# Batch 0's output projection in blocks of 384 and 192 tokens instead of two of 288

## The chip, the core and the metric

One core of a Trainium2 chip runs the whole program. The metric is device time in microseconds of one execution. The engines named below are PE (TensorE: matrix multiplies; its weight loads have a row of their own, PEld), DVE (VectorE), ACT (ScalarE), POOL (GpSimd) and SP (SyncE, which here only issues DMAs).

## The reference: what is computed

For 8 batches of 576 tokens, 8 heads and head width 64, attention reads a memory of 32 slots; the 4608 rows that come out go through a feed-forward network without a bias:

```
a      = softmax(phi over the 32 slots)
k_m    = a^T k,  v_m = a^T v            # per batch and head: 32 x 64
attn   = softmax(q k_m^T / 8) v_m       # 576 x 64 per head, 8 heads -> rows of 512
out    = ((attn @ w1) * (attn @ w2)) @ w3 @ w_out     # 512 -> 1024 -> 1024 -> 512
```

The output is float32, 4608 x 512; the kernel writes it transposed, as `outT` of 512 x 4608.

## The kernel before, in words

**Weights.** `w3` and `w_out` are multiplied together at the start (`product`, L435), so that one matrix of 1024 x 512 is left behind the product of the two first layers. It is held as a high and a low part in reduced float32, `Wh` and `Wl`.

**A batch** has two stages. In the first (`ab_unit`, L550 to L561; tokens A, a and g of the order strings) PE makes both first layers of one block of 128 features for one half of 288 tokens with 12 matmuls, ACT copies one of them out of PSUM (`a_sb`) and DVE multiplies the other with it into the tile `g`. There are 16 such units. In the second stage PE multiplies the result by `Wh` and `Wl`. For that each piece of `g` is split: ACT rounds it to the high part `sh` (token h, `high_part`, L589) and DVE subtracts to get the low part `sl` (token l, `low_part`, L595). Four buffers each of `sh` and `sl` are used in turn.

**Batch 0's second stage** is of another form than that of batches 1 to 7, and is the place of the change. It is made of 16 calls of `plain_unit` (token Q, L631), here called Q0 to Q15. Q0 to Q7 make the first half of the tokens, Q8 to Q15 the second; in each half the even ones make output rows 0 to 255 and the odd ones rows 256 to 511. A call is 12 matmuls: two column blocks of 128, two blocks of features, and three products each (`Wh` with `sh`, `Wl` with `sh`, `Wh` with `sl`). Every matmul loads 128 x 128 weights and streams 288 tokens past them. The first half accumulates in the two pairs of PSUM banks called ab, which attention also borrows, the second half in the pairs o and x. Tokens d0 to d3 (`plain_result`, L642) copy the four results out of PSUM on ACT into a tile `c` (3 buffers) and store it with one DMA from SP (`store`, L648).

**The order** is written out by hand: the strings FIRST (batch 0), SECOND and BATCH give the order in which steps are recorded, and every engine executes its own instructions in that order. Between the calls Q of batch 0 stand the steps of batch 1's attention: turn (PE transposes, L187, L190), mem (L206, L215), block (PE transposes, L234), M0 to M3 (products of the memory with `w1` and `w2`, L328, with Mh on ACT, L339, and Ml on DVE, L344), sc0 and sc1 (scores, L254), then a softmax on DVE and ACT up to `ah` and `al` (L298, L302), which batch 1's first stage reads. Behind Q15 come M2 (L328), then batch 1's first units. The buffer of PSUM that a step gets is picked when the program is made.

**SP's queue** is one line: it issues a DMA only when the tile to be stored is ready or the buffer to be filled is free, and what is behind it waits. Around d0 to d3 it holds the stores, the load of `kv` for batch 2 (four DMAs, L134 and L140) and that of `q` (L145).

Of the kernel before, what the change touches and what calls it, by code (L numbers as in the profile page):

```python
# [8 lines left out]
F32 = mybir.dt.float32  # L9
F32R = mybir.dt.float32r  # L10
# [4 lines left out]
ALU = mybir.AluOpType  # L15
# [14 lines left out]
FIRST = """  # L30
phi A a g A C1 M1 C2 C2 a g Mh1 Ml1 C3 C4 A A a g C1 a C5 g C4 C3 A A C5 a g C2 C1 a g M2 Mh2 C3 A a C4 Ml2 C1 g A C2
a C5 C4 A a g D0 A C3 g C5 A a g q h0 l0 kv Dt0 a g E0 M3 Mh3 Ml3 D1 Et0 F0 D3 A a Dt1 g D2 E1 A A Dt2 a g Et1 F1 E2 A
a g h1 l1 A a h3 g a g Et2 h2 l2 Dt3 Q E3 Q Q Et3 top h4 l3 Q l4 Q exp norm h5 Q l5 h6 turn0 l6 turn4 turnc4 Q turnc0
mem memc Q h7 l7 d0 Q kv block F3 d1 Q F2 blockc M0 b1 a0 sc0 scc0 mx0 Mh0 sb0 ex0 Ml0 Q Q Q M1 a2 sc1 Q sm0 mu0 Mh1
scc1 q a3 b0 tr0 ah0 Q Q d2 al0 a1 d3 Ml1
"""
# [20 lines left out]
def memory_attention__then__bilinear_ffn_kernel(  # L57
# [21 lines left out]
    nc = tc.nc  # L79
    P = 128  # L80
    B, NG, _, S = qT.shape
# [8 lines left out]
    HALF = S // 2  # L90
# [22 lines left out]
    def pair_ab():  # L113
        return ps_ab.tile([P, 2, 512], F32, name="ab")
# [328 lines left out]
    OH = DO // 2  # L443
# [91 lines left out]
    big = ctx.enter_context(tc.tile_pool(name="big", bufs=1, reuse_waits="tile"))  # L535
# [44 lines left out]
    order = (1, 4, 2, 6, 5, 7, 3)  # L580
    weights = {1: (0, 0), 5: (0, 1), 2: (1, 0), 3: (1, 1), 7: (2, 0), 6: (2, 1), 4: (3, 0)}
    sources = {1: (0, 0), 2: (0, 1), 6: (1, 1), 5: (0, 0), 7: (1, 0), 3: (0, 1), 4: (1, 1)}

    plain = ((0, 0), (0, 1), (1, 0), (1, 1))

    def high_part(b, m, G):
        src = G[sources[order[m // 2]] if b else plain[m // 2]][:, m % 2 * 2 : m % 2 * 2 + 2]
        hi = big.tile([P, 2, HALF], F32R, name="sh", tag="sh", bufs=4)
        nc.scalar.copy(out=hi, in_=src)  # L589
        G["X", m] = [hi, None, src]  # L590

    def low_part(b, m, G):
        hi, _, src = G["X", m]
        lo = G["X", m][1] = big.tile([P, 2, HALF], F32R, name="sl", tag="sl", bufs=4)
        nc.vector.tensor_tensor(out=lo, in0=src, in1=hi.bitcast(F32), op=ALU.subtract)  # L595

    def out_unit(b, m, G):
# [21 lines left out]
    def plain_unit(m, G):  # L619

        block, oh = m // 2, m % 2
        n, part = block // 4, block % 4
        if part == 0:
            G["C", n, oh] = (pair_o, pair_x)[oh]() if n else pair_ab()
        hi, lo, _ = G["X", block]
        for j in range(2):
            oc = slice(oh * OH + j * P, oh * OH + (j + 1) * P)
            for k in range(2):
                f = 2 * part + k
                for t, (x, y) in enumerate(((Wh, hi), (Wl, hi), (Wh, lo))):  # L630
                    nc.tensor.matmul(  # L631
                        G["C", n, oh][:, j, :HALF],
                        lhsT=x[f // half][:, f % half, oc],
                        rhs=y[:, k],
                        start=f == 0 and t == 0,
                        stop=f == NF - 1 and t == 2,
                    )

    def plain_result(i, G):
        n, oh = i // 2, i % 2  # L640
        c = big.tile([P, 2, HALF], F32, name="c", tag="c", bufs=3)
        nc.scalar.copy(out=c, in_=G["C", n, oh][:, :, :HALF])  # L642
        store(0, n, oh, c)

    def store(b, n, oh, c):
        at = b * S + n * HALF
        dst = outT[oh * OH : (oh + 1) * OH, at : at + HALF].rearrange("(j p) s -> p j s", j=2)
        nc.sync.dma_start(out=dst, in_=c)  # L648
# [21 lines left out]
    def batches():  # L670

        nonlocal n_o
        for b in range(B):
# [11 lines left out]
            for what in tokens((FIRST, SECOND, BATCH)[min(b, 2)]):  # L685
# [5 lines left out]
                elif what == "O":  # L691
                    out_unit(b, n_o, G)
                    n_o += 1
                elif what == "Q":
                    plain_unit(n_o, G)
                    n_o += 1
                elif what in at_stage:
                    next(next(at_stage[what]))
                elif key in ("M", "Mh", "Ml"):
                    at = b if in_a else b + 1  # L700
                    if at < B:
                        steps[at][what](pair_o if in_a and b else spare_bank(b, in_a))
                elif what in LOADS:
                    load(what + ("1" if what == "phi" or in_a else "2"), b)
                elif key == "h":
                    high_part(b, int(digit), G)
                elif key == "l":
                    low_part(b, int(digit), G)
                elif key == "f":
                    first_sum(int(digit), G)  # L710
                elif key == "S":
                    sums(what, G)
                elif key == "d":
                    plain_result(int(digit), G)
                elif what in ("p1", "p4", "p5", "u2"):
                    keep(what, G)
                elif key == "C":
                    result(b, what, G)
                elif key[0] == "-" or what in steps[0]:
                    at = b if key[0] == "-" else b + 1  # L720
                    if at < B:
                        steps[at][what.lstrip("-")](spare_bank(b, in_a))
                else:
                    weights_of_out(key, int(digit))
# [51 lines left out]
```

## Time and profile before

| | us |
|---|---|
| median of 3 runs (lowest, highest) | 541.66 (541.65, 544.39) |
| the profiled execution, its own time | 544.74 |
| its span, first to last instruction | 543.0 |
| mean granted TensorE clock | 0.993 |
| PE busy | 524.4 |
| PE weight loads busy | 445.5 |
| DVE, ACT, POOL busy | 358.8, 276.9, 127.7 |

The page is one execution. Busy time of PE counts pipelined matmuls whose durations overlap: a row's mean duration (about 295 ns for 288 tokens) is longer than the distance from one to the next. The chain of waits follows the work that ended last back through whatever released it, and gives stretches with their start and length. A timeline row has the start, the duration, engine, line, operation, output and inputs, shapes, a count, and in brackets the idle time before it with what ended that. Rows of SP's queue are marked SPq; the DMA view gives the time from a DMA's issue to its landing.

### The profile page before, as it was taken

The numbers are of one execution on the slowest core, as the hardware profiler recorded it, in microseconds if no ns is written. First come the engines' busy times: TensorE is split into PE (matmuls) and PEld (weight loads), VectorE is DVE, ScalarE is ACT, GpSimd is POOL, SyncE is SP. The second block draws the span as 40 slices with busy tenths as digits, with TensorE's granted clock in tenths as the row PEclk, the third lists the DMA queues.
The fourth block names the chain that finished last, engine by engine and source line by source line (L and its number), as shares of the span: only waits on it lengthen the run. The fifth ranks groups of instructions, "written<-read, shape, count | busy, mean of one in ns | idle before, by whom it ended". The sixth has DMA issues, their size and how long they took to land.

```text
span 543.0 us, 10835 instructions
## 1 busy us (share of the span) xinstructions
PE 524.4 (97%) x4528; PEld 445.5 (82%) x4528; DVE 358.8 (66%) x588; ACT 276.9 (51%) x469; POOL 127.7 (24%) x142
## 2 busy tenths in 40 slices
PE   2998998999999999999999999999999999999997
PEld 1444457898899898989998899889997989899996
DVE  4874958863654895389555975498548853896464
ACT  5887528644655534555354544453455345553342
POOL 0005000110163702070015302350217020800180
PEclk9997999999999999999999999999999999999999
DMA  8999712704511323043305330531123310011001
GB/s 313 404 409 357 293 43 78 262 0 164 187 45 74 125 80 118 1 176 125 95 1 175 110 109 2 174 112 66 45 91 120 140 45 1 2 45 45 1 23 65
DMA packets 28303, 64.12 MB, mean 118 GB/s; under 512 B 1632, under 2 KB 9824, under 8 KB 28256
## 3 DMA queue, kind: packets, MB, share of 16 engines
q1 hardware_dynamic: 28256, 63.45, 33.4%
q8 instruction: 35, 0.57, 0.4%
q14 instruction: 12, 0.10, 0.1%
HBM read 54.00 MB, written 9.44 MB: 117 GB/s over the span
## 4 chain that ended last, share of the span: by engine, by line
PE 89%; DMA 7%; ACT 2%; DVE 1%; SPq 1%; issue 0%
PE ab L550 37%; PE x L610 13%; PE o L610 13%; PE ab L610 4%; DMA kv<-in_kv 3%; PE ab L328 3%; PE x L435 3%; PE o L328 3%; PE o L435 3%; PE ab L631 2%; PE x L206 2%; DMA raw<-in_w_out 2%; PE ab L254 2%; PE x L631 1%; PE o L631 1%; DMA raw<-in_w3T 1%
## 5 line engine op out<-in xcount | busy, mean ns | idle before, releaser
L550 PE MATMUL ab<-ah,mh 128*128 128x288 f32 x512 | 154.6, 302 | 1.8 <-DVE ml L344 1.8
L550 PE MATMUL ab<-al,mh 128*128 128x288 f32 x512 | 151.1, 295 | 0.0
L550 PE MATMUL ab<-ah,ml 128*128 128x288 f32 x512 | 151.1, 295 | 0.0
L561 DVE TENSOR_TENSOR g<-ab,a_sb 128x288 f32<-128x288 f32 x128 | 58.0, 453 | 104.8 <-ACT a_sb L559 103.8
L550 PEld LDWEIGHTS ab<-ah,mh 128*128 128x128 f32 x512 | 96.2, 188 | 18.3 <-DVE g L561 8.5
L559 ACT COPY a_sb<-ab 128x288 f32<-128x288 f32 x128 | 50.9, 398 | 109.4 <-PE ab L550 105.9
L595 DVE TENSOR_TENSOR sl<-g,sh 128x576 fp32r<-128x576 f32 x106 | 86.6, 831 | 20.1 <-ACT sh L589 19.9
L550 PEld LDWEIGHTS ab<-al,mh 128*128 128x128 f32 x512 | 96.3, 188 | 0.2 <-issue 0.2
L550 PEld LDWEIGHTS ab<-ah,ml 128*128 128x128 f32 x512 | 96.3, 188 | 0.0
L589 ACT CAST sh<-g 128x576 fp32r<-128x576 f32 x106 | 71.0, 675 | 44.4 <-PE x L610 17.9
L566 POOL TENSOR_TENSOR g<-g,g 128x288 f32<-128x288 f32 x28 | 22.2, 807 | 155.0 <-DVE g L561 154.7
L574 POOL TENSOR_TENSOR g<-g,g 128x288 f32<-128x288 f32 x28 | 28.1, 1023 | 107.0 <-ACT a_sb L559 80.5
L610 PE MATMUL o<-sh,Wh 128*128 128x288 f32 x168 | 50.6, 301 | 0.0
L610 PE MATMUL x<-sh,Wh 128*128 128x288 f32 x168 | 50.5, 300 | 0.0
L610 PE MATMUL o<-sh,Wl 128*128 128x288 f32 x168 | 49.6, 295 | 0.0
L610 PE MATMUL x<-sh,Wl 128*128 128x288 f32 x168 | 49.6, 295 | 0.0
L610 PE MATMUL x<-sl,Wh 128*128 128x288 f32 x168 | 49.6, 295 | 0.0
L610 PE MATMUL o<-sl,Wh 128*128 128x288 f32 x168 | 49.5, 295 | 0.0
L435 PE MATMUL ab<-wo,w 128*128 128x512 f32 x64 | 29.8, 621 | 10.0 <-DVE wo L424 10.0
L610 PEld LDWEIGHTS x<-sh,Wh 128*128 128x128 f32 x168 | 31.6, 188 | 7.0 <-issue 7.0
L610 PEld LDWEIGHTS o<-sh,Wh 128*128 128x128 f32 x168 | 31.6, 188 | 3.6 <-issue 3.6
L435 PEld LDWEIGHTS ab<-wo,w 128*128 128x128 f32 x64 | 12.5, 201 | 25.3 <-issue 14.3
(139 smaller groups left out, 951.8 us busy)
## 6 DMA issues: line engine op xcount, KB each, us to landing
kv<-in_kv SPq DMA_DIRECT2D x16, 1024.0 KB, 7.4
q<-in_qT SPq DMA_DIRECT2D x8, 1152.0 KB, 5.9
outT<-c SPq DMA_DIRECT2D x32, 288.0 KB, 2.3
raw<-in_w3T SPq DMA_DIRECT2D x7, 1024.0 KB, 14.8
ph<-in_phiT SPq DMA_DIRECT2D x8, 576.0 KB, 3.8
raw<-in_w SPq DMA_DIRECT2D x4, 1024.0 KB, 18.2
raw<-in_w_out SPq DMA_DIRECT2D x3, 1024.0 KB, 10.4
kv<-in_w SPq DMA_DIRECT2D x3, 1024.0 KB, 10.9
```

Source lines behind the costliest of these rows:

```text
L206: nc.tensor.matmul(ps[h * M : (h + 1) * M, t, : 2 * D], lhsT=v["a"][:, i, t, h * M : (h + 1) * M], rhs=kvt[i][:, (4 * t + h) * 2 * D : (4 ...
L328: nc.tensor.matmul(ps[g * M : (g + 1) * M, t], lhsT=vm[b % 2][d, g], rhs=w12_sb[q][d, :, g], start=True, stop=True,)
L435: nc.tensor.matmul(pw[r][i], lhsT=x[:, i * P : (i + 1) * P], rhs=wos[k // half][:, k % half], start=k == 0, stop=k == NF - 1,)
L550: nc.tensor.matmul(both[:, w, :HALF], lhsT=x[:, t, w, fc : fc + P], rhs=y[:, n, t * HALF : (t + 1) * HALF], start=i == 0, stop=i == len(to ...
L559: nc.scalar.copy(out=a_sb, in_=both[:, 0, :HALF])
L561: nc.vector.tensor_tensor(out=G[n, f // half][:, f % half], in0=both[:, 1, :HALF], in1=a_sb, op=ALU.mult)
L566: nc.gpsimd.tensor_tensor(out=low, in0=top, in1=low, op=ALU.subtract)
L574: gp(out=s2, in0=s2, in1=s3, op=ALU.subtract)
L589: nc.scalar.copy(out=hi, in_=src)
L595: nc.vector.tensor_tensor(out=lo, in0=src, in1=hi.bitcast(F32), op=ALU.subtract)
L610: nc.tensor.matmul(ps[:, j, :HALF], lhsT=x[s][:, 2 * part + k, jc], rhs=y[:, k], start=i in (1, 4, 2, 5) and part == 0 and k == 0 and t == ...
L631: nc.tensor.matmul(G["C", n, oh][:, j, :HALF], lhsT=x[f // half][:, f % half, oc], rhs=y[:, k], start=f == 0 and t == 0, stop=f == NF - 1 ...
```

## The change

Batch 0's second stage is cut after 384 tokens instead of after 288. Q0 to Q7 stream 384 tokens in each matmul, Q8 to Q15 stream 192. The number of matmuls and of weight loads stays 192.

The first stage still makes `g` in halves of 288 tokens. So each of the first four pieces of `sh` and `sl` is now put together from two sources, 288 tokens of the first half and 96 of the second, with two instructions on ACT and two on DVE instead of one each; the last four pieces hold 192 tokens and take one each. The buffers of `sh` and `sl` are 384 wide in all batches; batches 1 to 7 use 288 of each 384.

The results are copied and stored one column block of 128 rows at a time: eight copies on ACT (four of 384, four of 192) and eight DMAs (192 KB and 96 KB) instead of four copies of 576 and four DMAs of 288 KB. The three buffers of `c` remain. In FIRST the step h3 moves behind two g, since it now reads what they write.

```diff
-a g h1 l1 A a h3 g a g Et2 h2 l2 Dt3 Q E3 Q Q Et3 top h4 l3 Q l4 Q exp norm h5 Q l5 h6 turn0 l6 turn4 turnc4 Q turnc0
+a g h1 l1 A a g a g h3 Et2 h2 l2 Dt3 Q E3 Q Q Et3 top h4 l3 Q l4 Q exp norm h5 Q l5 h6 turn0 l6 turn4 turnc4 Q turnc0
...
-    plain = ((0, 0), (0, 1), (1, 0), (1, 1))
+    WIDE = 384
+
+    def plain_parts(m, G):
+
+        fh, ks = m % 4 // 2, slice(m % 2 * 2, m % 2 * 2 + 2)
+        if m < 4:
+            return [(0, G[0, fh][:, ks]), (HALF, G[1, fh][:, ks, : WIDE - HALF])]
+        return [(0, G[1, fh][:, ks, WIDE - HALF :])]
 
     def high_part(b, m, G):
...
+        if b == 0:
+            parts = plain_parts(m, G)
+            hi = big.tile([P, 2, WIDE], F32R, name="sh", tag="sh", bufs=4)
+            for at, src in parts:
+                nc.scalar.copy(out=hi[:, :, at : at + src.shape[2]], in_=src)
+            G["X", m] = [hi, None, parts]
+            return
...
     def low_part(b, m, G):
...
+            for at, x in src:
+                x_at = slice(at, at + x.shape[2])
+                nc.vector.tensor_tensor(out=lo[:, :, x_at], in0=x, in1=hi[:, :, x_at].bitcast(F32), op=ALU.subtract)
+            return
...
     def plain_unit(m, G):
...
+        width = S - WIDE if n else WIDE
...
-                        G["C", n, oh][:, j, :HALF],
+                        G["C", n, oh][:, j, :width],
                         lhsT=x[f // half][:, f % half, oc],
-                        rhs=y[:, k],
+                        rhs=y[:, k, :width],
...
     def plain_result(i, G):
         n, oh = i // 2, i % 2
-        c = big.tile([P, 2, HALF], F32, name="c", tag="c", bufs=3)
-        nc.scalar.copy(out=c, in_=G["C", n, oh][:, :, :HALF])
-        store(0, n, oh, c)
+        at, width = (WIDE, S - WIDE) if n else (0, WIDE)
+        for j in range(2):
+            c = big.tile([P, 2, HALF], F32, name="c", tag="c", bufs=3).rearrange("p j s -> p (j s)")[:, :width]
+            nc.scalar.copy(out=c, in_=G["C", n, oh][:, j, :width])
+            nc.sync.dma_start(out=outT[oh * OH + j * P : oh * OH + (j + 1) * P, at : at + width], in_=c)
```

How the instructions stand then is shown at three places. A name in brackets says which engine's or DMA queue's count an instruction waits for (Activation is ACT, DMAHW the DMAs, each number one of their counters); `ab`, `o`, `x` are PSUM, `c` the result tile.

ACT at d0 and d1, with the rounding h7 ahead of them and the first of the `moved` copies behind; before:

```order
L589 CAST sh<-g_487 128x576 [waits PE_49]
L642 COPY c<-ab 128x576
L642 COPY c<-ab 128x576 [waits PE_49]
L453 COPY moved<-raw_685 128x2x256 [waits PE_49]
L453 COPY moved<-raw_86 128x512 [waits Pool_49]
```

and with the change:

```order
L598 CAST sh<-g_487 128x2x192 [waits PE_49]
L666 COPY c<-ab 128x384 x2
L666 COPY c<-ab 128x384 [waits PE_49]
L666 COPY c<-ab 128x384 [waits DMAHW2_49,Activation_49]
L453 COPY moved<-raw_685 128x2x256 [waits PE_49]
```

Two copies became four, and the fourth, which takes the buffer of the first, waits for a DMA: the store of that first copy.

ACT at d2 and d3 and what is behind them (L339 is Mh2, L457 a rounding of `w_out`'s part, L559 the first `a_sb` of batch 1); before:

```order
L298 CAST ah<-at 128x576 [waits DVE_49]
L642 COPY c<-o 128x576 [waits PE_49]
L453 COPY moved<-raw_86 128x512 [waits PE_49,Activation_49]
L642 COPY c<-x 128x576 [waits DMAHW2_49,PE_49,Activation_49]
L339 CAST mh_1253<-o 128x1024 [waits PE_49]
L457 CAST Wh_82<-raw_87 128x256
L559 COPY a_sb<-ab 128x288 [waits PE_49]
```

and with the change:

```order
L298 CAST ah<-at 128x576 [waits DVE_49]
L666 COPY c<-o 128x192 [waits DMAHW3_49,PE_49,Activation_49]
L666 COPY c<-o 128x192 [waits DMAHW0_49,Activation_49]
L453 COPY moved<-raw_86 128x512 [waits PE_49]
L666 COPY c<-x 128x192 [waits DMAHW1_49,PE_49,Activation_49]
L666 COPY c<-x 128x192 [waits DMAHW3_49,Activation_49]
L339 CAST mh_1273<-o 128x1024 [waits PE_49]
L457 CAST Wh_82<-raw_87 128x256
L559 COPY a_sb<-ab 128x288 [waits PE_49]
```

Each of the four copies waits for a DMA; the last takes the buffer of the first of these four and waits for its store, which was issued just before. Before, the one copy that waits for a DMA waits for d0's store.

PE at M0 and sc0, behind Q9; before:

```order
L631 MATMUL x<-sl,Wh_82 128x288
L328 MATMUL ab<-w_0_78,vm_77 32x512 [waits DVE_49,Activation_49]
L328 MATMUL ab<-w_0_78,vm_77 32x512 [waits DVE_49]
L328 MATMUL ab<-w_0_78,vm_77 32x512 x6
L254 MATMUL ab<-q,km_75 32x288 [waits DMAHW5_49,PE_49]
L254 MATMUL ab<-q,km_75 32x288 x7
```

and with the change:

```order
L653 MATMUL x<-sl,Wh_82 128x192
L328 MATMUL ab<-w_0_78,vm_77 32x512 [waits DVE_49,PE_49]
L328 MATMUL ab<-w_0_78,vm_77 32x512 x7
L254 MATMUL ab<-q,km_75 32x288 [waits DMAHW5_49,Activation_49]
L254 MATMUL ab<-q,km_75 32x288 x7
```

The PSUM buffer that d1 empties goes to sc0 (L254) instead of M0 (L328), so the wait for ACT's copies moves from the one to the other.

More of the change, by code (lines that the diff above doesn't have):

```diff
@@ L582, in memory_attention__then__bilinear_ffn_kernel @@
     sources = {1: (0, 0), 2: (0, 1), 6: (1, 1), 5: (0, 0), 7: (1, 0), 3: (0, 1), 4: (1, 1)}
-    plain = ((0, 0), (0, 1), (1, 0), (1, 1))
-    def high_part(b, m, G):
-        src = G[sources[order[m // 2]] if b else plain[m // 2]][:, m % 2 * 2 : m % 2 * 2 + 2]
-        hi = big.tile([P, 2, HALF], F32R, name="sh", tag="sh", bufs=4)
+    WIDE = 384
[4 more added lines that the diff above has]
+        return [(0, G[1, fh][:, ks, WIDE - HALF :])]
+    def high_part(b, m, G):
+        if b == 0:
[5 more added lines that the diff above has]
+            return
+        src = G[sources[order[m // 2]]][:, m % 2 * 2 : m % 2 * 2 + 2]
+        hi = big.tile([P, 2, WIDE], F32R, name="sh", tag="sh", bufs=4)[:, :, :HALF]
         nc.scalar.copy(out=hi, in_=src)
@@ L593, in low_part @@
         hi, _, src = G["X", m]
-        lo = G["X", m][1] = big.tile([P, 2, HALF], F32R, name="sl", tag="sl", bufs=4)
+        lo = big.tile([P, 2, WIDE], F32R, name="sl", tag="sl", bufs=4)
+        if b == 0:
+            G["X", m][1] = lo
+            for at, x in src:
+                x_at = slice(at, at + x.shape[2])
+                nc.vector.tensor_tensor(out=lo[:, :, x_at], in0=x, in1=hi[:, :, x_at].bitcast(F32), op=ALU.subtract)
+            return
+        lo = G["X", m][1] = lo[:, :, :HALF]
         nc.vector.tensor_tensor(out=lo, in0=src, in1=hi.bitcast(F32), op=ALU.subtract)
```

## The prediction, as written before the result was known

> **What bounds the kernel now.** I read the page's busy times first, then the chain of waits around batch 0's second stage, then single rows of PE, ACT, DVE and the DMAs there.
>
> ```profile
> PE 524.4 (97%) x4528; PEld 445.5 (82%) x4528; DVE 358.8 (66%) x588; ACT 276.9 (51%) x469; POOL 127.7 (24%) x142
> ...
> 111.01 9.52 PE ab L631 x72
> 120.54 0.87 PE o L187 x8
> ...
> 125.38 1.79 PE ab L631 x12
> 127.17 1.59 PE o L631 x12
> ...
> 133.86 1.59 PE x L631 x12
> ...
> 141.91 1.59 PE x L631 x12
> 143.50 1.02 PE o L328 x16
> ```
>
> PE is busy 97% of the span, and from Q0 to batch 1's first units the chain is PE alone, without a gap: 72 matmuls of 288 tokens in 9.52 us, 132.2 ns each (I use 132.3, since a call takes 1.59). So any time added to a matmul here is added to the end, and any wait of PE too. Whether something behind could absorb it, the same view says: its rows stay on PE to the end. What matters is then how a matmul's spacing depends on its tokens, and which new wait reaches PE.
>
> **The change part by part.**
>
> *Wide and narrow matmuls.* 96 matmuls go from 288 to 384 tokens, 96 from 288 to 192. The tokens' sum is the same, so if the spacing were proportional to tokens, or a constant plus a part per token, the change would cost nothing. Other widths, of other kinds of matmul, are in these rows:
>
> ```profile
> 36.33 0.59 PE L435 MATMUL ab<-wo,w 128*128 128x512 f32 x1
> 36.87 3.60 PE L435 MATMUL ab<-wo,w 128*128 128x512 f32 x8
> ...
> 120.37 1.04 PE L187 MATMUL o<-ident,ph 128*128 128x128 f32 x8
> 121.25 0.27 PE L190 MATMUL x<-ident,ph 128*128 128x128 f32 x1
> ...
> 132.01 0.19 PEld L631 LDWEIGHTS o<-sh,Wh 128*128 128x128 f32 x1 [0.47 <-issue]
> 132.12 0.19 PEld L631 LDWEIGHTS o<-sh,Wl 128*128 128x128 f32 x1
> 132.25 0.19 PEld L631 LDWEIGHTS o<-sl,Wh 128*128 128x128 f32 x1
> ```
>
> Eight float32 matmuls of 512 take 3.60, less the last one's 0.59, over seven: 430 ns apart. Eight transposes of 128: (1.04 - 0.27)/7 = 110 ns. The line through both has 0.83 ns a token and 3 ns fixed. Reduced float32 is faster; if it streams at twice that rate (an estimate), 288 tokens take 120 of the 132.3 ns and 12.5 are fixed. Then 384 tokens take 172 ns. Bounds: 176 if all of 132.3 is proportional, 160 if the fixed part is hidden in a long matmul (384 x 0.415). I take 172, the case with a fixed part, since the two float32 rows have one too.
>
> For 192 tokens the same line gives 92 ns, but each matmul also needs its own load of 128 x 128 weights. In the last three rows the first load of a call begins at 132.01 and the second at 132.12, though the first matmul had nothing before it: 0.11 us for a load when nothing else holds it up; later loads follow at the matmuls' 0.13. The transposes, a load each, are 0.11 apart too. So I take 110 ns for the narrow matmul, limited by its load, not its tokens. Bounds: 92 below (load free), 163 above (192 at the float32 rows' 0.83 ns, plus 3).
>
> Sum: 96 x (172.3 - 132.3) = +3.84 us in Q0 to Q7, 96 x (110 - 132.3) = -2.14 us in Q8 to Q15, together **+1.70 us**.
>
> The Trainium skill, "TensorE: Matmul & The Clock Gate", section "LDWEIGHTS (loading the stationary operand)", prices a load at its columns over 1.2 GHz, 107 ns for 128; that speaks against narrow matmuls, and the trace's 110 agrees. Its section "Back-to-back issue gap" gives the bare spacing as tokens over 2.4 GHz plus 2.5 ns; by it 384 and 192 tokens take 162.5 + 82.5 = 245 ns, as much as two of 288, so the change would cost nothing. The trace's 132.3 instead of its 122.5 at 288 tokens does not bear it out.
>
> *More instructions on ACT and DVE.* The roundings h and subtractions l of the first four pieces take a second instruction of 192 elements each, h3 is later, and the copies are halved.
>
> ```profile
> 104.00:111.00 7.00, 6.59 (x50) 6.59 (x51) 5.37 (x12) 3.21 (x8) 0.74 (x1) 1.00 0.30 94
> ...
> 130.62 1.14 ACT L453 COPY moved<-raw 128x512 f32<-128x512 f32 x2 [1.79 <-PE x L631]
> ```
>
> What hides it: in the last 7 us of the first stage (busy times of PE, PEld, DVE, ACT in that order) DVE leaves 1.6 us and ACT 3.8, and Q4, the first to need h2, starts four wide calls after the last unit. I cost this at nothing; uncovered, it would be four extra instructions of about 0.3 us on ACT, 1.2 us. That batches 1 to 7 now write 288 of every 384 elements costs nothing: of the two `moved` copies in 1.14 us one writes 2 x 256 elements to a wider tile, the other 512 in one piece.
>
> *d0 and d1: the store of the first copy.* With three buffers of `c` the fourth copy waits until the first store has landed, and sc0 on PE now waits for that copy.
>
> ```profile
> 121.56 0.27 ACT L198 COPY a<-x 128x128 f32<-128x128 f32 x1 [0.39 <-PE x L190]
> ...
> 127.07 0.67 ACT L589 CAST sh<-g 128x576 fp32r<-128x576 f32 x1 [0.91 <-PE ab L631]
> 127.65 1.18 ACT L642 COPY c<-ab 128x576 f32<-128x576 f32 x2
> ...
> 141.95 0.64 ACT L642 COPY c<-o 128x576 f32<-128x576 f32 x1
> ...
> 128.31 0.39 SPq L648 DMA_DIRECT2D outT<-c  x1
> 128.82 0.94 SPq L134 DMA_DIRECT2D kv<-in_kv  x2
> ...
> 131.39 0.69 PE L254 MATMUL ab<-q,km 64*32 64x288 f32 x16
> ...
> DMA to landing us min/median/max: 2.2/2.3/9.1
> ```
>
> A copy of 576 takes 0.64, one of 128 takes 0.27: 0.83 ns an element, so 384 take 0.48 and 192 take 0.32. Q7's end is 3.84 later; h7 starts at 130.9, the first copy at about 131.3, its store at 131.8, landing 2.2 to 2.8 later (2.8 is the store at 128.31, by its own row below), at 134.0 to 134.6; the fourth copy ends 0.5 after that, 134.5 to 135.1. sc0 would start at 131.39 + 3.84 - 2 x 12 x 0.0223 = 134.7. Stall between 0 and 0.4 us; I take **0.1**, nearer the early end, since this store has two thirds of the bytes of d0's. Uncovered on ACT: `moved` and Mh0 start some 0.7 later, but Ml0 waits for DVE's softmax steps anyway.
>
> *d2 and d3: the store of the fifth copy.* The eighth copy waits for the store of the fifth, issued one call earlier, and behind the eighth copy on ACT stand Mh2, a rounding, and the first `a_sb` of batch 1, for which DVE and then PE wait.
>
> ```profile
> outT<-c SPq DMA_DIRECT2D x1, 288.0 KB, 2.8
> ...
> outT<-c SPq DMA_DIRECT2D x1, 288.0 KB, 9.1
> ...
> 138.65 0.37 SPq L145 DMA_DIRECT2D q<-in_qT  x1
> 142.62 2.41 SPq L648 DMA_DIRECT2D outT<-c  x2
> ...
> q<-in_qT SPq DMA_DIRECT2D x1, 1152.0 KB, 5.8
> ...
> outT<-c SPq DMA_DIRECT2D x1, 288.0 KB, 3.6
> ```
>
> These are the landing times of the stores at 128.31 and 131.12, of the load of `q` at 138.65, and of the store at 142.62. d1's store, behind `kv`, took 9.1; d2's, behind `q`, took 3.6 and landed at 146.2, 1.8 after `q` (144.4). So stores come after the loads ahead of them. (The sixth and seventh copies wait for d1's two stores, which land about 131.12 + 9.1 + 3.84 = 144.1; they are due at 144.4 and later, so I price these waits at nothing.)
>
> Now the clock after: `q` is issued when sc1 is done, 138.65 + 3.84 - 5 x 0.268 + 0.1 = 141.25, and lands at 147.05. The fifth copy is made at about 144.3; its store (a third of the bytes) lands 0.6 to 1.8 after `q`, I take 0.95: 148.0. The chain on ACT from there:
>
> ```profile
> 143.99 0.63 ACT L642 COPY c<-x 128x576 f32<-128x576 f32 x1
> 144.63 1.02 ACT L339 CAST mh<-o 128x1024 fp32r<-128x1024 f32 x1
> 145.54 0.41 ACT L457 CAST Wh<-raw 128x256 fp32r<-128x256 f32 x1
> 146.35 0.40 ACT L559 COPY a_sb<-ab 128x288 f32<-128x288 f32 x1 [0.40 <-PE ab L550]
> ...
> 146.78 0.46 DVE L561 TENSOR_TENSOR g<-ab,a_sb 128x288 f32<-128x288 f32 x1 [1.46 <-ACT a_sb L559]
> 147.16 1.21 DVE L344 TENSOR_TENSOR ml<-o,mh 128x1024 fp32r<-128x1024 f32 x1
> ...
> 152.71 0.76 DVE L302 TENSOR_TENSOR al<-at,ah 128x576 fp32r<-128x576 f32 x1 [0.40 <-ACT ah L298]
> 153.52 0.46 DVE L561 TENSOR_TENSOR g<-ab,a_sb 128x288 f32<-128x288 f32 x1
> ...
> 154.08 0.35 PE L550 MATMUL ab<-ah,mh 128*128 128x288 f32 x1
> ```
>
> Copy 0.32, Mh2 0.91 to the next start, the rounding 0.35: `a_sb` at 149.6. PE alone would allow 146.35 + 1.70 + 0.1 = 148.15. It is 1.45 late; with landings from 0.6 to 1.8 behind `q`, 1.1 to 2.3. And nothing absorbs it: from the first `g` at 146.78 DVE works without a pause up to 152.71, where it waits for ACT's `ah`, itself made from DVE's work, and the seventh unit's first matmul at 154.08 lasts 0.35 instead of 0.29, so PE waits there already. I take **1.4**.
>
> Sum: 1.7 + 0.1 + 1.4 = **+3.2 us**. The profiled execution has 544.74 and a span of 543.0; it would become 547.9, with a span near 546.2. It was itself 3.1 above the median of the runs shown, 541.66, so I put the difference on the median: **544.9 us**.
>
> **The rivals.**
>
> *No price for the load.* If narrow matmuls take 92 ns, the sum of the matmuls is 0. But what Q8 and Q9 gain is lost again, since the fourth copy still ends at 134.6 or later and holds sc0: sc0 at 134.7 is 3.3 later than before, sc1 3.3 - 3 x 0.48 = 1.9 later, `q` and the fifth store follow it, and `a_sb` comes 2.5 late instead of 3.2: 544.2. The Trainium skill's bare spacing, above, would give the same sum. For it: the tokens add up to the same. Against it: 0.11 between two loads.
>
> *The last store is not late (the other side: not slower).* If the fifth copy's store lands in the usual 2.3 after its issue at about 144.4, at 146.6, the eighth copy is done in time for `a_sb` at 148.15 and only 1.8 remains: 543.5, within 0.5% of before. It decides from a landing of 146.6 on, earlier changes nothing. For it: the median of 32 stores is 2.3. Against it: the two rows of 9.1 and 3.6.
>
> *Narrow matmuls run at float32's rate.* At 163 ns: 96 x (172 + 163 - 264.6) = +6.8 us, 548.5, and the stores then have time to land. For it: only that no row has a reduced float32 matmul under 288 tokens. Against it: nothing in the order or shapes makes them float32.
>
> That the change doesn't do what it says is excluded by the order: 128x384, 128x192, the same number of matmuls.
>
> **How the numbers follow.** Forecast 50% (544.9; its own range, with the bounds 160 to 176 for wide matmuls inside the stall, 543.4 to 546.4), no price for the load 17% (544.2), last store not late 18% (543.5), float32's rate 8% (548.5), the rest 7%, split between a gain that I don't see and a longer stall. A measurement of this kernel can tell about 0.5%, 2.7 us, from no change, so slower means above 544.4: of the forecast 70%, of the first rival 40%, the third whole, with half of the rest, 0.35 + 0.07 + 0.08 + 0.04 and 0.02 for the second, 0.56. Within: 0.40. Faster: 0.04. The range leaves out a tenth on each side: 542.2 to 548.6.
>
> **What would show it.** PE rows: wide calls of 2.07 us (12 x 172), narrow ones of 1.32 (12 x 110); 1.1 if the load is free, 1.96 at float32's rate. ACT: a fourth copy that waits for a DMA and an eighth that waits for one 2 us or more after the seventh. PE: an idle stretch of 1 to 2 us spread over batch 1's first seven units, waiting for DVE's `g`. The prediction is wrong if the eighth copy waits for PE rather than a DMA, if a wide call takes under 1.95, or if PE waits in the first stage for `g`, which I cost at nothing.

## The result, and the profile after

The change makes the kernel slower: 547.67 us (median, 546.9 to 549.88) against 541.79 (541.4 to 544.39), a ratio of 1.0105 with a 95% interval of 1.0082 to 1.0127. The forecast was 544.9; the cost is 5.9 us and not 3.2.

The profiled execution of the kernel before took 2.9 us longer than others ahead of Q0 (it reaches Q0 at 110.85 us, the kernel after at 107.95); of the profiled executions below, one does the same (320 and 256 tokens, 110.87). So all stretches below are counted from the start of Q0 to the end: 432.11 us before, 437.96 after, **+5.85**.

The page's busy times, after:

```profile
PE 526.4 (96%) x4528; PEld 447.7 (82%) x4528; DVE 359.1 (66%) x592; ACT 277.3 (51%) x477; POOL 127.6 (23%) x142
```

PE is busy 2.0 us longer than before (524.4), less than the kernel lost: part of the loss is work, part is waiting. Where, the chain of waits after shows (start, length, what):

```profile
108.11 12.58 PE ab L653 x72
...
121.67 2.08 PE ab L653 x12
...
128.67 0.40 ACT c L666 x2
129.07 2.98 DMA outT<-c
...
132.14 0.49 ACT c L666
...
132.67 0.72 PE ab L254 x16
133.39 1.52 PE o L653 x12
134.91 1.34 PE x L653 x12
...
142.15 0.33 ACT c L666 x2
142.48 4.21 DMA outT<-c
...
146.77 0.32 ACT c L666
147.08 0.92 ACT mh L339
148.00 0.30 ACT Wh L457
148.30 0.31 ACT a_sb L559
...
148.63 0.47 DVE g L561
...
149.15 8.59 PE ab L550 x60
```

Before, this stretch of the chain was PE alone. Now it leaves PE twice, both times through a store of `c`: at 129.07 to sc0 (L254), which waits for the copy that waits for the first store, and at 142.48 to batch 1's first units (L550), which wait for `g`, `a_sb`, Mh2 and the eighth copy, in that order back. PE's list of waits after (engine, line, for what: us, times, longest) gives both stalls:

```profile
PE ab L550 <- DVE g L561: 1.7, 2, 1.5
...
PE ab L254 <- ACT c L666: 0.4, 1, 0.4
```

Neither row is in the list of before. The rows count only from the end of the matmul before, and the first distance from start to start behind a stall is longer too (0.24 us against 0.13), so the losses in the table below are counted from start to start. Three views of after around d3 follow: ACT's rows, the issue of `q` on SP's queue, and the DMAs with their median time from issue to landing:

```profile
143.73 0.31 ACT L666 COPY c<-x 128x192 f32<-128x192 f32 x1
146.77 0.32 ACT L666 COPY c<-x 128x192 f32<-128x192 f32 x1 [2.72 <-DMA outT<-c]
146.98 1.02 ACT L339 CAST mh<-o 128x1024 fp32r<-128x1024 f32 x1
```

```profile
139.19 0.39 SPq L145 DMA_DIRECT2D q<-in_qT  x1
```

```profile
q<-in_qT SPq DMA_DIRECT2D x1, 1152.0 KB, 6.4
...
outT<-c SPq DMA_DIRECT2D x4, 96.0 KB, 3.6
```

The eighth copy starts 3.04 us after the seventh and waits 2.72 of them.

No wait shows a third part, which lies behind all this. The out matmuls of batches 1 to 7 became slower, though the change did not touch their widths. Here are the last stage of batch 7 in the chain of before and then of after (24 matmuls a row):

```profile
516.74 3.17 PE o L610 x24
519.91 3.17 PE x L610 x24
523.09 3.17 PE ab L610 x24
```

```profile
519.47 3.20 PE o L631 x24
522.67 3.20 PE x L631 x24
525.87 3.20 PE ab L631 x24
```

Over all such distances from one start to the next (1124 in each trace, those with a call's edge or a wait left out) the mean went from 132.31 to 133.21 ns. Batches 1 to 7 have 1176 out matmuls: 0.90 x 1176 = 1.06 us.

Set against the stretches of PE from Q0 on, the loss stands like this. The price of the widths and the split of the two waits come from the experiments below.

| | us |
|---|---|
| batch 0's out matmuls, at their new widths | +1.96 |
| sc0 waits for the fourth copy (start of batch 1's first units, 36.28 instead of 35.58 behind Q0) | +0.70 |
| batch 1's first 84 matmuls wait for the eighth copy (13.43 us instead of 11.36) | +2.07 |
| out matmuls of batches 1 to 7 | +1.06 |
| rest | +0.06 |
| sum | +5.85 |

### The profile page after: what moved, and what is told of

Same layout as the page of the kernel before. It is cut to its first block, busy times and chain, and to the rows that moved or that the text cites. A ratio compares the mean times of both kernels' runs of the same rounds, so it can differ in the third digit from the quotient of the medians.

```text
span 545.9 us, 10860 instructions
## 1 busy us (share of the span) xinstructions
PE 526.4 (96%) x4528; PEld 447.7 (82%) x4528; DVE 359.1 (66%) x592; ACT 277.3 (51%) x477; POOL 127.6 (23%) x142
## 4 chain that ended last, share of the span: by engine, by line
PE 87%; DMA 8%; ACT 2%; DVE 1%; SPq 1%; issue 0%; ACTq 0%
PE ab L550 36%; PE x L631 13%; PE o L631 13%; PE ab L631 4%; DMA kv<-in_kv 3%; PE ab L328 3%; PE ab L653 3%; PE o L435 3%; PE x L435 3%; PE o L328 2%; PE x L206 2%; DMA raw<-in_w_out 2%; PE ab L254 2%; DMA outT<-c 1%; DMA raw<-in_w3T 1%; PE x L187 1%
## 5 line engine op out<-in xcount | busy, mean ns | idle before, releaser
L550 PE MATMUL ab<-ah,mh 128*128 128x288 f32 x512 | 154.9, 303 | 3.3 <-DVE g L561 1.7
L550 PE MATMUL ab<-al,mh 128*128 128x288 f32 x512 | 151.1, 295 | 0.0
L550 PE MATMUL ab<-ah,ml 128*128 128x288 f32 x512 | 151.0, 295 | 0.0
L550 PEld LDWEIGHTS ab<-ah,mh 128*128 128x128 f32 x512 | 96.2, 188 | 20.3 <-DVE g L561 10.7
L559 ACT COPY a_sb<-ab 128x288 f32<-128x288 f32 x128 | 50.9, 398 | 108.9 <-PE ab L550 105.4
L550 PEld LDWEIGHTS ab<-al,mh 128*128 128x128 f32 x512 | 96.3, 188 | 0.2 <-issue 0.2
L550 PEld LDWEIGHTS ab<-ah,ml 128*128 128x128 f32 x512 | 96.3, 188 | 0.0
L616 DVE TENSOR_TENSOR sl<-g,sh 128x576 fp32r<-128x576 f32 x98 | 80.6, 837 | 12.2 <-ACT sh L603 12.2
L603 ACT CAST sh<-g 128x576 fp32r<-128x576 f32 x98 | 65.6, 674 | 39.5 <-PE x L631 18.2
```

The source lines that it names most:

```text
L550: nc.tensor.matmul(both[:, w, :HALF], lhsT=x[:, t, w, fc : fc + P], rhs=y[:, n, t * HALF : (t + 1) * HALF], start=i == 0, stop=i == len(to ...
L559: nc.scalar.copy(out=a_sb, in_=both[:, 0, :HALF])
```

## The experiments

All medians stand against the same kernel before, run beside them (541.8 to 541.9 in each comparison).

| run | median us | ratio to before, 95% interval | Q0 to end, against 432.11 |
|---|---|---|---|
| buffers 384 wide, nothing else | 543.28 | 1.0025 (1.0007 to 1.0044) | +1.21 |
| after, second block copied once | 545.67 | 1.0071 (1.005 to 1.0092) | +3.27 |
| after, both blocks copied once | 544.83 | 1.0047 (1.0031 to 1.0063) | +3.02 |
| after, slices side by side | 546.30 | 1.0084 (1.0064 to 1.0104) | +4.52 |
| after, `q` loaded last | 545.73 | 1.0071 (1.0048 to 1.0094) | +3.62 |
| widths alone, 384 and 192 | 543.76 | 1.0027 (1.001 to 1.0043) | +1.96 |
| widths alone, 320 and 256 | 541.63 | 0.999 (0.9973 to 1.0008) | -0.25 |
| 432 and 144 | 546.70 | 1.0079 (1.0052 to 1.0105) | +4.56 |
| places of the slices by batch | 542.07 | 1.0001 (0.9982 to 1.002) | +0.27 |
| a second set of places, one execution | 542.25 | none | +0.54 |
| before, all slices at byte 128 | 540.02 | 0.9966 (0.9948 to 0.9984) | -1.77 |

### The buffers' width alone

```diff
 # kernel before
-        hi = big.tile([P, 2, HALF], F32R, name="sh", tag="sh", bufs=4)
+        hi = big.tile([P, 2, 384], F32R, name="sh", tag="sh", bufs=4)[:, :, :HALF]
...
-        lo = G["X", m][1] = big.tile([P, 2, HALF], F32R, name="sl", tag="sl", bufs=4)
+        lo = G["X", m][1] = big.tile([P, 2, 384], F32R, name="sl", tag="sl", bufs=4)[:, :, :HALF]
```

> Kernel before with one edit: the sh and sl buffers are 384 tokens wide and used by 288 of them, in all batches, as the change leaves them. Theory (the layout of the buffers slows the out matmuls of batches 1 to 7): their spacing goes from 132.3 to 133.2 ns as in the kernel after, 1344 x 0.9 ns = +1.2 us, so about 543.0 us. Rival (the 1.1 us that the kernel after loses behind batch 1 comes from the order or from ACT's extra instructions): spacing stays 132.3 ns, 541.8 us.

Measured: +1.21 us from Q0, and the spacing is that of the kernel after, 133.21 ns. In its chain, batch 7:

```profile
515.18 3.20 PE o L610 x24
518.38 3.20 PE x L610 x24
```

So the edit that the prediction priced at nothing costs over a microsecond by itself. (The expectation counts 1344 matmuls; it is 1176 in batches 1 to 7 and 192 in batch 0, which are padded here too and go from 132.37 to 133.17 ns: 1.06 + 0.15 = 1.21.)

### The copies of the second block

```diff
 # kernel after, plain_result
+        if n:
+            c = big.tile([P, 2, HALF], F32, name="c", tag="c", bufs=3)[:, :, :width]
+            nc.scalar.copy(out=c, in_=G["C", n, oh][:, :, :width])
+            nc.sync.dma_start(out=outT[oh * OH : (oh + 1) * OH, at : at + width].rearrange("(j p) s -> p j s", j=2), in_=c)
+            return
```

> Kernel after with one edit: the results of the second block (192 tokens) are copied and stored as in the kernel before, one copy of both column blocks into one c and one store each, so d2 and d3 need two c buffers and not four, and no copy there waits for a store just issued. Theory (the eighth copy waits for the fifth copy's store, and the first units of batch 1 for the product behind it): that wait goes, the first 84 matmuls of batch 1 take 11.4 us and not 13.4, and the kernel about 547.7 - 2.0 = 545.7 us. Rival (ACT is behind with the split copies themselves): the 13.4 us stay, 547.5 us.

Measured: 545.67 us, and batch 1's first 84 matmuls take 11.36 us. PE's waits of this run:

```profile
PE ab L328 <- DVE g L561: 0.2, 1, 0.2
PE ab L550 <- DVE g L561: 0.2, 1, 0.2
```

The 1.7 us before L550 are down to 0.2. That shows the split copies of d2 and d3, which need four buffers where there are three, as the cause. It does not yet say why the store was late.

### The copies of both blocks

```diff
 # kernel after
+    def c_tile(width):
+        c = big.tile([P, 2 * WIDE], F32, name="c", tag="c", bufs=3)
+        return c[:, : 2 * width].rearrange("p (j s) -> p j s", j=2)
...
 # plain_result, for both blocks
+        c = c_tile(width)
+        nc.scalar.copy(out=c, in_=G["C", n, oh][:, :, :width])
+        nc.sync.dma_start(out=outT[oh * OH : (oh + 1) * OH, at : at + width].rearrange("(j p) s -> p j s", j=2), in_=c)
```

> Kernel after with both blocks' results copied and stored once each, from c buffers of 2 x 384: no copy waits for a store just issued. Theory: the 2.0 us of the run above, and besides the fourth copy's wait, which delays sc0 by 0.4 to 0.6 us: 547.7 - 2.5 = 545.2 us, with ACT's row of a c copy waiting for a DMA gone around sc0. Rival (sc0 waits for something else at ACT): 545.7 us, the same as the run above.

Measured: 544.83 us. In the chain of this run the stretch is PE alone again, and sc0 follows M0 at once:

```profile
130.77 1.02 PE ab L328 x16
131.79 0.49 PE ab L254 x16
132.28 1.51 PE o L653 x12
```

Batch 1's first units start 35.58 us behind Q0, in the run before this one 35.97, in the kernel after 36.28. So the fourth copy's wait costs 0.4 to 0.7 us; it varies between the two runs that have it, whose instructions are the same up to there, by just as much as the landing of the first store (2.67 us behind the copy and 2.98). From Q0 to the end the split copies cost 437.96 - 435.13 = 2.83 us.

### Both slices side by side

```diff
 # kernel after, batches 1 to 7
-        hi = big.tile([P, 2, WIDE], F32R, name="sh", tag="sh", bufs=4)[:, :, :HALF]
+        hi = big.tile([P, 2, WIDE], F32R, name="sh", tag="sh", bufs=4).rearrange("p k s -> p (k s)")
+        hi = hi[:, : 2 * HALF].rearrange("p (k s) -> p k s", k=2)
 # and the same for lo
```

> Kernel after with one edit: in batches 1 to 7 the 288 tokens of both slices of sh and sl lie side by side in the 384-wide buffer (1152 bytes from slice to slice, not 1536); the buffers' first addresses stay as in the kernel after. Theory A (the distance of the slices matters): the out matmuls of batches 1 to 7 go back from 133.2 to 132.3 ns, 546.5 us. Theory B (the first addresses of the buffers matter: all 64 above a multiple of 512, where before every second was 320 above one): spacing stays 133.2 ns, 547.7 us. Between them: half of it, 132.7 ns.

Measured: 546.30 us, out matmuls at 132.31 ns, theory A. In the chain, batch 7:

```profile
518.14 3.17 PE o L633 x24
521.31 3.17 PE x L633 x24
```

The buffers' first addresses did not move, only the second slice inside each, from 1536 to 1152 bytes behind the first. So it is not the padding's extra space, nor what ACT and DVE write, but where the matmul finds its second operand.

### The load of q behind the stores

```diff
 # kernel after, end of FIRST
-scc1 q a3 b0 tr0 ah0 Q Q d2 al0 a1 d3 Ml1
+scc1 a3 b0 tr0 ah0 Q Q d2 al0 a1 d3 q Ml1
```

> Kernel after with one edit: the load of q (1152 KB) is put on SP's queue behind the eight stores and not ahead of the last four. Theory (the fifth copy's store lands 4.2 us after its issue, and not the usual 2.3, because q's load is ahead of it in the queue): it lands about 2.3 us after its issue, the eighth copy waits 0.8 us instead of 2.7, the first 84 matmuls of batch 1 take 11.4 to 11.6 us instead of 13.4, and the kernel 547.7 - 1.9 = 545.8 us. Rival (small stores of a column block land late of themselves): 4 us again, 547.6 us.

Measured: 545.73 us, batch 1's first 84 matmuls in 11.37 us. ACT's rows and the DMAs of this run:

```profile
143.52 0.76 ACT L666 COPY c<-x 128x192 f32<-128x192 f32 x2
144.20 1.02 ACT L339 CAST mh<-o 128x1024 fp32r<-128x1024 f32 x1
```

```profile
outT<-c SPq DMA_DIRECT2D x4, 96.0 KB, 1.7
```

The eighth copy follows the seventh without a pause. The same four stores land 1.7 us after their issue (median), and not 3.6. The first of them is the one that counts: it took 4.2 and takes 1.6. Small stores are not slow (in the kernel after, the eighth copy's store, issued at 147.11 when `q` had landed, took 1.6 too); this one stood behind a load of 1152 KB. The Trainium skill, "DMA: Bandwidth & Descriptors", section "Two DMAs through the same engine are not ordered", says that in one queue of one DMA engine descriptors start in order, though they are pipelined; the two traces fit that, 4.2 us with `q` ahead and 1.6 without. Whether the store waited for its turn or shared what moves the data with the load, these two runs do not tell apart.

### The widths alone

The kernel with both mends, one copy per block and slices side by side.

> Kernel after with the results copied and stored once per block (as in the third run) and the 288 tokens of both slices side by side in batches 1 to 7 (as in the fourth): only the widths of batch 0's out matmuls are left of the change, and the split copies into sh and sl. Theory: the widths alone, 96 x (174.3 - 132.4) - 96 x (132.4 - 111.4) = 4.02 - 2.01 = +2.0 us over the kernel before, 543.8 us. Rival (the two mends overlap, or something else is left): 544.8 us, as with the copies alone.

Measured: 543.76 us, +1.96 from Q0. Spacings: 174.33 ns at 384 tokens (91 distances), 111.49 at 192 (89), 132.30 in batches 1 to 7. So 96 x (174.33 - 132.37) - 96 x (132.37 - 111.49) = 4.03 - 2.00 = +2.02, all that is left. (Not quite all of it is width: in batch 0 the two slices still lie 1536 bytes apart, and at that place 288 tokens take 133.17 ns and not 132.37, as the first run showed. Of the 4.03, 96 x 0.8 ns = 0.08 us are then the place's, an estimate; what the place does at 192 tokens, no run shows.) The instructions that ACT and DVE make more of for the split pieces cost nothing that can be seen: the sum of the widths leaves no room for them.

### Other widths

The same kernel with 320 and 256 tokens:

```diff
-    WIDE = 384
+    WIDE = 320
```

> The run above with blocks of 320 and 256 tokens. Theory (spacing is linear in the tokens, 0.437 ns per token through 288 and 384, until the load of the next weights sets a floor of 111 ns): 146.3 and 118.4 ns, sum 96 x (13.9 - 14.0) = 0.0 us, 541.8 us. Rival (below 288 the spacing falls by the slope from 288 to 192, 0.218 ns per token, with no floor): 146.3 and 125.4 ns, +0.7 us, 542.5 us.

and with 432 and 144, with the copies of the second experiment:

```diff
-    WIDE = 384
+    WIDE = 432
```

> Blocks of 432 and 144 tokens, with the slices side by side in batches 1 to 7; the first block's results copied and stored per column block as in the kernel after (the buffers for one copy of it have no room), the second's once. Theory (floor): 195.3 and 111.4 ns, 96 x (62.9 - 21.0) = +4.0 us, with 0.3 to 0.5 us for the fourth copy's wait 546.2 us. Rival (slope of 0.218 ns per token below 288): 195.3 and 100.9 ns, +3.0 us, 545.2 us.

Rows of the chain, first of 320 and 256, then of 432 and 144:

```profile
111.03 10.56 PE ab L655 x72
...
140.59 1.36 PE o L655 x12
```

```profile
108.11 14.12 PE ab L655 x72
...
137.04 1.34 PE x L655 x12
```

| tokens | 144 | 192 | 256 | 288 | 320 | 384 | 432 |
|---|---|---|---|---|---|---|---|
| spacing, ns | 111.2 | 111.5 | 115.8 | 132.4 (133.2) | 146.7 | 174.3 | 196.3 |

The slices of the kernels with 320 and 384 lie 1280 and 1536 bytes apart, at one place modulo 256 as in the first run, whose 133.17 ns at 288 stand in brackets. From there to 384 it is (174.33 - 133.17) / 96 = 0.429 ns per token with 9.7 ns fixed, which gives 146.9 at 320, close to the run; at 432, where the places change from buffer to buffer, it gives 194.9 and the run 196.3. 144 and 192 tokens cost the same, a floor of 111 ns, which rules out the rival's slope (100.9 at 144). The Trainium skill, "TensorE: Matmul & The Clock Gate", section "LDWEIGHTS (loading the stationary operand)", would put a load at 107 ns, columns over 1.2 GHz; the floor here is 4 ns above that. That the load sets the floor is argued from this nearness; no run has narrow matmuls without loads of their own. At 256 the line gives 119.4 and the run 115.8. So 320 and 256 come out a little below two of 288 (96 x (14.3 - 16.5) = -0.2 us, no difference that the times can tell). Why 256 lies below the line is open.

So no cut tried here wins by the widths: a part under some 240 tokens (an estimate, where the line meets the floor: (111 - 9.7) / 0.429 = 236) pays the floor and not its tokens, and above that the two changes nearly cancel. The 432 and 144 run pays 96 x 64.0 - 96 x 21.2 = +4.11 for its widths. Batch 1's first units start 4.80 us later there than before (38.40 against 33.60 behind Q0), which leaves 0.69 for sc0's wait; the whole loss is 4.56 counted from Q0 and 4.9 in the medians.

### Where the slices lie

Now to the layout. Of the kernel before, with 768-element buffers and another place for the two slices in each batch:

```diff
+    layout = ((0, 288), (0, 288), (0, 384), (0, 320), (16, 320), (48, 336), (112, 304), (0, 304))
+
+    def slices(b, tag):
+        at, step = layout[b]
+        x = big.tile([P, 2 * 384], F32R, name=tag, tag=tag, bufs=4)
+        return x[:, at : at + 2 * step].rearrange("p (k s) -> p k s", k=2)[:, :, :HALF]
```

> Kernel before with sh and sl in 768-element buffers and another place of the two slices in each of the batches 1 to 7; their first bytes modulo 512, in order of the batches: 64 and 192 (as in the kernel before, for a yardstick), 64 and 64 (as in the kernel after), 64 and 320, 128 and 384, 256 and 64, 0 and 192, 64 and 256. Read by the spacing of each batch's out matmuls. Theory (a matmul is slower when its operand begins at the same place modulo 256 as the one ahead): 132.3, 133.2, 133.2, 133.2, 132.3, 132.3, 132.3 ns. Rival A (modulo 512): 132.3, 133.2, 132.3, 132.3, 132.3, 132.3, 132.3 ns. Rival B (the distance of 1536 bytes itself): only the second slow. A layout below 132.0 ns would be one to use throughout.

and a second set of places, with those of the ab matmuls' operands too:

```diff
+    places = ((0, 288), (0, 320), (0, 320), (0, 320), (16, 320), (16, 320), (48, 320), (32, 320))
+
+    def probs_tile(b, x):
+        at, step = places[b]
+        y = att.tile([P, 1408], F32R, name=x, tag=x)[:, at : at + 4 * step]
+        return y.rearrange("p (n t s) -> p n t s", n=2, t=2)[:, :, :, :HALF]
```

> As the layouts run, with other places, and with the places of ah and al (the attention's two parts, the operands of the ab matmuls) set by batch as well. First bytes modulo 256 of the two slices of sh and sl, batches 1 to 7: 0 and 0, 192 and 192, 128 and 0, 0 and 128, 128 and 64, 128 and 192, 128 and 128. Theory (it is the place modulo 128 of each slice: the layouts run had 131.7 ns at 128 and 128, 133.2 at 64 and 64): 131.7, 133.2, 131.7, 131.7, 132.5, 132.5, 131.7 ns. Rival (only 128 and 128 is fast, for a reason of its own): 131.7 in the last batch alone. The ab matmuls, whose slices stand at 64 and 192 in the kernel before (132.4 ns), get 64 and 64 in batches 1 to 3, 128 and 128 in 4 and 5, 0 and 0 in 6, 192 and 192 in 7: 133.2, 131.7, 131.7 and 133.2 ns if the same rule holds for them, 132.4 throughout if it is a matter of the out matmuls alone.

Mean spacing of the out matmuls of one batch each (158 to 166 distances), by the first bytes of the two slices modulo 256:

| first, second | ns | first, second | ns |
|---|---|---|---|
| 64, 192 (as before) | 132.31 | 0, 0 | 133.30 |
| 64, 64 (as after) | 133.19 | 192, 192 | 131.66 |
| 64, 64 (modulo 512: 64, 320) | 133.18 | 128, 0 | 133.07 |
| 128, 128 | 131.71 | 0, 128 | 133.27 |
| 128, 128 (another address) | 131.67 | 128, 64 | 132.64 |
| 0, 64 | 132.96 | 128, 192 | 132.16 |
| 0, 192 | 132.24 | 64, 0 | 132.21 |

For the ab matmuls: 64 and 192 (before) 132.33, 64 and 64 133.18, 128 and 128 131.62, 0 and 0 133.30, 192 and 192 132.22. Three rows of 72 ab matmuls from the chain of the second run, at 64 and 64, at 128 and 128, at 0 and 0 (each holds the longer distances between units too, so only their differences count: 0.12 us over 72 is 1.7 ns):

```profile
261.74 9.79 PE ab L557 x72
...
319.54 9.67 PE ab L557 x72
...
434.65 9.79 PE ab L557 x72
```

Every theory on record fell in part. "The same place modulo 256 is slow" fails at 128 and 128, the fastest; "modulo 512" fails at 64 and 320; the distance of 1536 bytes is not needed, since 1280 is as slow; "modulo 128" fails at 0 and 0. What holds: two slices at 0 or at 64 are slow (133.2 to 133.3), two at 128 fast (131.6 to 131.7), in out and ab matmuls alike. At 192 and 192 the out matmuls are fast and the ab matmuls are not, and 0 and 64 differs from 64 and 0, so two places do not make the whole rule. It stays open.

### All slices at byte 128

```diff
 # kernel before, with the functions of the second set of places
+    layout = ((16, 320),) * 8      # sh, sl: 64 + 4 x 16 = 128 modulo 256
+    places = ((16, 320),) * 8      # ah, al
```

> Kernel before (two blocks of 288) with every slice of sh, sl, ah and al beginning at byte 128 modulo 256, the layout with the shortest spacing so far. Theory (131.7 and not 132.3 ns for 1536 out and 1536 ab matmuls): 3072 x 0.6 ns = -1.8 us, 540.0 us. Rival A (the out matmuls alone): -0.9 us, 540.9 us. Rival B (the spacing of one batch said nothing of a whole kernel): 541.8 us.

Measured: 540.02 us, ratio 0.9966 (0.9948 to 0.9984): faster than both kernels, by 1.9 us and by 7.6. In the chain of its last stage:

```profile
512.20 3.16 PE o L624 x24
515.36 3.16 PE x L624 x24
```

The spacings are 131.6 to 131.7 ns in every batch, for out and ab. With the true counts, 1368 out matmuls x 0.65 and 1536 ab x 0.7 = 2.0 us, against 1.9 in the medians; the 1344 ab matmuls behind Q0 make it 1.8, against 1.77 from Q0. (The expectation counts 1536 out matmuls.)

## Why the prediction was right or wrong

The direction and both of the waits it named were right. Point by point:

- **Wide matmuls**: taken at 172.3 ns, measured 174.3 (bounds 160 to 176). Of the 2.0 ns that were missing, 0.8 come with the buffers (last point): the step started from 132.3, and at the new place 288 tokens take 133.17. The other 1.2 are the split, 12.5 ns fixed and 0.416 per token by the estimate of twice float32's rate, 9.7 and 0.429 by the widths above. Cost +4.03 us and not +3.84.
- **Narrow matmuls**: taken at 110, measured 111.4, and the floor shown at two widths. -2.0 and not -2.14. The sum of both, 1.70, is 1.96 to 2.02. The rivals "no price for the load" (92 ns) and "float32's rate" (163 ns) are out.
- **More instructions on ACT and DVE**: nothing, as said.
- **d0 and d1**: sc0 waits for the fourth copy, as said, but 0.4 to 0.7 us and not 0.1. The step chose the early end of its range because the store is smaller; the store landed 2.98 us after the copy, above the 2.8 taken as the late end.
- **d2 and d3**: the mechanism is as told, `q`'s load ahead of the fifth copy's store, and is shown by moving `q`. The term was 1.4 and measured 2.07, inside its bounds of 1.1 to 2.3. `q` was taken to need 5.8 us, the time before, and needed 6.4; the store landed 1.1 us behind it (142.48 + 4.21 against 139.19 + 6.4) where 0.95 was taken. The rival "the last store is not late" is what happens when `q` is not ahead.
- **Buffers 384 wide in batches 1 to 7**: this is the step that failed. It was priced at nothing by looking at the instructions that write the buffers, the two `moved` copies; that PE reads them 1176 times was not asked. It costs 1.06 us there, and some 0.08 more inside the wide matmuls' term, by the estimate above.

Of the 2.65 us by which the sum was short, 1.06 come from that last step, 0.67 from batch 1's first units, 0.60 from sc0 and 0.26 from the widths. The forecast's own range, up to 546.4, missed the time; the whole range, up to 548.6, holds it. That is luck in part: its upper end comes from the rival at 548.5, float32's rate, which did not happen; the time came near it for other reasons.

What the prediction said would show: narrow calls of 1.32 us are there (1.34), the eighth copy waits for a DMA and starts 3.04 us after the seventh, PE waits 1.7 us in batch 1's first units for `g`. A wide call takes 2.08, against 2.07.

## What to carry to other kernels

Where one engine is the bound, a change is priced by everything that engine reads, not only by what is written anew: a wider buffer moved an operand and cost 0.7% on each of 1176 matmuls, which no wait shows, only the distance from start to start. Splitting a result into more pieces over the same few buffers turns a store's landing time into a wait; ask what stands ahead of that store in its queue, and put a large load behind it. And a matmul with its own weights was not worth narrowing below the floor of its spacing, here 111 ns, close to what a load takes, or some 240 tokens.

## What was not expected of the hardware

- The spacing of the same matmul depends on where its moving operand begins: 131.6 to 133.3 ns at 288 tokens, by the first byte modulo 256. At 64 and 64 single distances alternate between 130 and 136 or 137 ns, at 64 and 192 most lie between 131 and 134. Moving the operands to 128 made the kernel 0.34% faster.
- Between 144 and 192 tokens the spacing does not move (111.2, 111.5 ns), at 256 it is 115.8, 3.6 below the line through 288 and 384.
